# A frequency-filter and mixture-of-experts kernel: six PSUM banks and thinner gating steps in the forward part, expert products in column halves of 64

## The chip, the cores and the metric

The kernel runs on one core of a Trainium2 chip. The metric is the device time of one execution in microseconds; a kernel's time is the median of its runs. The engines are named as in the profile: PE is the matrix engine (PEld its weight loads), DVE the vector engine, ACT the scalar engine, POOL the GpSimd engine, SP the engine that issues most DMAs.

## The reference

Two blocks follow each other. The first multiplies the spectrum of each sequence by a filter, the second sends each row to one of eight experts, of which each takes at most 80 rows.

```python
# x: (8, 2496, 256), filt: (1249, 256) complex
X = np.fft.rfft(x, axis=1)
y = np.fft.irfft(X * F[None], n=2496, axis=1).reshape(19968, 256)
logits = y @ w_gate                      # (256, 8)
expert_idx = np.argmax(logits, axis=1)
probs = softmax(logits)                  # gate_w: the chosen expert's share
for e in range(8):
    tok_idx = np.where(expert_idx == e)[0]
    if len(tok_idx) > 80:                # keep the 80 of the largest gate_w
        tok_idx = tok_idx[np.argpartition(-gate_w[tok_idx], 80)[:80]]
    h = np.maximum(y[tok_idx] @ w1[e], 0.0)          # (80, 256) @ (256, 1024)
    out[tok_idx] = gate_w[tok_idx, None] * (h @ w2[e])   # (80, 1024) @ (1024, 256)
# all other rows of out are zero
```

## The kernel before

The transform of length 2496 is done as 39 times 64 points by products with tables. All matrices are float32, and the trace shows two passes of the PE for each float32 product (a call of 16 products appears as x32). The program has three parts, written out in one order by hand; each engine works through its own instructions in that order.

**Forward part** (a loop over k = 0..79; ten steps make a batch b, r is the step within it). One step holds, on PE, `turn_t(k+1)` (4 transposes, L322, copied by ACT), `stage2(k)` (4 products with the second table, L334) and one piece of `stage1` (L308, copied by ACT L313). DVE makes two products `p` with the filter (L340) of stage 2's result, POOL adds and subtracts them into the spectrum `yt` (L348), and DVE transposes the spectrum for storage (L361). At r = 0 `gates(b-1)` (L385) multiplies the finished spectra of a batch by the gate matrix: 32 columns of weights at a time, in four column strips of the PE. At r = 0 `stage2(k)` stands behind stage 1 and the gates, at all other r ahead of stage 1. `turn_z` (L397) and `logits` follow at r = 2 to 4. For two batches at a time, a *gating* makes softmax and candidates in seven parts (`GATING`: for the third pair of batches at k = 67, 68, 69, 70, 72, 74, 75): maximum `mx` and difference `sh` (DVE L440, L442), exponential `ex` (ACT L444), `first`, `fm`, sum and reciprocal, the key, its transposes `pk` (L475) and the eight largest. Beside it run steps on the first four batches: threshold (k = 54 to 60), `ranks` (62), `codes` (63), lists (64, 65), `row_index` (69, a product of 64 little matrices, L664), `gather_rows` (70 to 73, POOL, L799) and `turn_rows` (75 to 78, DVE, L809). The PSUM of this part is a ring of five banks (`fps`), two banks for gates, `turn_z` and indices (`zps`), one for the rest (`mps`).

**Middle part.** Eight tiles of 128 chosen rows are transformed back: POOL gathers table rows (L799), DVE transposes them (`wt`, L809), and `fill(n)` issues the next n of the 20 products per tile (L816) against a page with the batch's spectrum. Between these stand the last two batches' gating, the final threshold, ranks, lists, `row_index` and the slots.

**Experts.** For each e: `turn(e+2)` (two transposes, L1094), `layer1(e+1)` (16 products of a 128 by 128 weight tile with the 80 rows, L1105), `layer2(e)` (8 products in which the hidden rows are the weights and 256 columns of w2 move, L1119), the scaling by ACT (L1122) and a scatter by POOL (L1124). Layer 1 of expert e+1 stands ahead of layer 2 of expert e. Weights of experts 5 to 7 are loaded once layer 2 of experts 0 to 2 has freed their buffers.

Of the kernel before, what the change touches and what calls it, by code (L numbers as in the profile page):

```python
# [91 lines left out]
def kernel(  # L92
# [158 lines left out]
    with tc.manual_schedule():  # L251
# [10 lines left out]
        fps = pool("fps", 5, PSUM)  # L262
        zps = pool("zps", 1, PSUM)
        mps = pool("mps", 1, PSUM)
# [63 lines left out]
        def stage2(k):  # L328
            h, g = divmod(k, NG)
            cb = h % NDB  # L330
            ps = fps.tile([128, SG, 2, NQ], F32, name=f"pb_{k}", tag="f")
            t = t2.pop(k)
            for i in range(SG):
                nc.tensor.matmul(out=ps[:, i].rearrange("p r q -> p (r q)"), lhsT=t[:, i, :],  # L334
                                 rhs=d_t[:, SG * g + i, :], start=True, stop=True)
            pr = []
# [43 lines left out]
        def gates(b):  # L380
            ps = zps.tile([128, 1024], F32, name=f"pz_{b}", tag="z")
            for p0, pn in ((0, 4), (4, 1)):
                for cb in range(NDB):
                    for j in range(4):
                        nc.tensor.matmul(  # L385
                            out=ps[32 * j:32 * j + 32, 128 * p0:128 * (p0 + pn)].rearrange(
# [4 lines left out]
            st["zt"] = gp.tile([128, 5, 128], F32, name=f"zt_{b}", tag="zt")  # L391
            nc.scalar.copy(out=st["zt"][:].rearrange("p t q -> p (t q)"), in_=ps[:, 0:640])

        def turn_z(b):
            ps = zps.tile([128, 8, 128], F32, name=f"py_{b}", tag="z")
            for t in range(5):
                nc.tensor.transpose(ps[:, t, :], st["zt"][:, t, :], ident[:])  # L397
            for e in range(0, E, 4):
                nc.scalar.copy(
                    out=zs[:, e:e + 4, 0:NS].rearrange("p e (j t) -> p t j e", t=5),  # L400
                    in_=ps[:, 0:5].rearrange("p t (j e) -> p t j e", e=EW)[:, :, :, e:e + 4])
# [24 lines left out]
        def gating(p, part):  # L426
# [11 lines left out]
            if part == 0:  # L438
                mx = row("mx")
                nc.vector.tensor_reduce(out=mx[:], in_=l, axis=AX.X, op=AL.max)  # L440
                st["sh"] = big("sh")
                nc.vector.tensor_tensor(out=st["sh"][:], in0=l, in1=bc(mx[:]), op=AL.subtract)  # L442
                st["ex"] = big("ex")
                nc.scalar.activation(out=st["ex"][:], in_=st["sh"][:], func=AF.Exp)  # L444
            elif part == 1:
# [4 lines left out]
                    op0=AL.is_equal, op1=AL.mult)  # L450
                st["fm"] = row("fm")
                nc.vector.tensor_reduce(out=st["fm"][:], in_=st["first"][:], axis=AX.X,
                                        op=AL.max)
            elif part == 2:
                gw = row("gw")
                nc.vector.tensor_reduce(out=gw[:], in_=st["ex"][:], axis=AX.X, op=AL.add)
                nc.vector.tensor_scalar(out=gw[:], in0=gw[:], scalar1=1e-9, scalar2=None,
                                        op0=AL.add)
                st["gw"] = row("gwr")
                nc.vector.reciprocal(out=st["gw"][:], in_=gw[:])  # L460
            elif part == 3:
# [3 lines left out]
                nc.vector.tensor_tensor(out=key[:, 0:N1, :], in0=oh[:], in1=bc(st["gw"][:]),  # L465
                                        op=AL.mult)
# [5 lines left out]
            elif part == 4:  # L472
# [6 lines left out]
            else:  # L479
                for i in (part - 5,):  # L480
# [4 lines left out]
                if part == 6:  # L485
# [109 lines left out]
        def codes(nb, kept, poff):  # L595
# [13 lines left out]
            nc.vector.max(out=cc[:, 8:16], in_=ff)  # L609
            ci = spt([128, KR], I32, "ci")  # L610
# [46 lines left out]
        def row_index(b0, nb):  # L657
            bn = nb - b0
            bplc, bval = st["bplc"], st["bval"]
            pz = zps.tile([128, 2, 512], F32, name=f"pb_r{nb}", tag="z")  # L660
            pb = pz[:, 0, 0:8 * bn].rearrange("p (v g b) -> p v g b", v=2, g=4)
# [16 lines left out]
            st["pz"] = pz  # L678
# [19 lines left out]
        def slot_lists():  # L698
            eplc, eval_ = st["eplc"], st["eval"]
            pe = st["pz"][:, 1, 0:4 * E].rearrange("p (v e) -> p v e", v=4)  # L700
# [180 lines left out]
        for p, steps in ((0, (25, 26, 27, 28, 30, 32, 33)), (1, (45, 46, 47, 48, 50, 52, 53)),  # L881
                         (2, (67, 68, 69, 70, 72, 74, 75))):
            for part, at in enumerate(steps):
                GATING[at] = p, part

        def early(k):
            if k in GATING:
                gating(*GATING[k])
# [741 lines left out]
```

## Time and profile before

| | us |
|---|---|
| median of 3 runs (436.3, 440.12, 451.39) | 440.12 |
| the profiled execution's own time | 442.61 |
| its span in the trace | 440.7 |
| PE busy | 386.9 (88%) |
| PE weight loads busy (beside PE) | 344.3 (78%) |
| DVE busy | 241.0 (55%) |
| POOL busy | 185.0 (42%) |
| ACT busy | 131.5 (30%) |

The forward part takes about the first 262 us of the span, the middle part runs to 372, the experts' products to 429, and the last scatters end the span. A row of the timeline gives the start and length of a run of like instructions, their count, and in brackets how long the engine had stood still before it and which instruction ended that. Lengths of single PE instructions overlap (the next begins while one drains), so the pace is read from starts, not from lengths.

### The profile page before, as it was taken

The numbers are of one execution on the slowest core, as the hardware profiler recorded it, in microseconds if no ns is written. First come the engines' busy times: TensorE is split into PE (matmuls) and PEld (weight loads), VectorE is DVE, ScalarE is ACT, GpSimd is POOL, SyncE is SP. The second block draws the span as 40 slices with busy tenths as digits, with TensorE's granted clock in tenths as the row PEclk, the third lists the DMA queues.
The fourth block names the chain that finished last, engine by engine and source line by source line (L and its number), as shares of the span: only waits on it lengthen the run. The fifth ranks groups of instructions, "written<-read, shape, count | busy, mean of one in ns | idle before, by whom it ended". The sixth has DMA issues, their size and how long they took to land. (4 is left out here: it accounts for less than half of the span.)

```text
span 440.7 us, 8021 instructions
## 1 busy us (share of the span) xinstructions
PE 386.9 (88%) x3047; PEld 344.3 (78%) x3047; DVE 241.0 (55%) x543; ACT 131.5 (30%) x264; POOL 185.0 (42%) x256
## 2 busy tenths in 40 slices
PE   3969999999999999999979959987939999999990
PEld 3969989898799887988977944776837888989870
DVE  7036567578697677887995792287554410110100
ACT  1524454444454443534443510210130000111110
POOL 7024445354355444553482877030444733401010
PEclk9999999999999999999998988998987999999996
DMA  7998699989889899999789584979499985397000
GB/s 214 215 207 288 162 330 311 311 258 305 267 193 333 242 283 275 357 317 329 189 239 340 161 313 134 312 270 409 147 385 396 348 259 200 78 330 233 9 18 10
DMA packets 42836, 109.95 MB, mean 249 GB/s; under 512 B 5354, under 2 KB 16232, under 8 KB 40920
## 3 DMA queue, kind: packets, MB, share of 16 engines
q1 hardware_dynamic: 37638, 99.03, 70.4%
q0 software_dynamic: 3728, 9.15, 6.4%
q10 hardware_dynamic: 1426, 1.19, 0.8%
q8 instruction: 26, 0.43, 0.4%
q14 instruction: 18, 0.15, 0.1%
HBM read 71.66 MB, written 40.58 MB: 255 GB/s over the span
## 5 line engine op out<-in xcount | busy, mean ns | idle before, releaser
L348 POOL TENSOR_TENSOR yt<-p,p 128x256 f32<-128x256 f32 x160 | 115.7, 746 | 132.5 <-DVE p L340 126.9
L340 DVE TENSOR_TENSOR p<-pb,ft 128x512 f32<-128x512 f32 x160 | 102.1, 679 | 60.9 <-PE pb L334 31.1
L308 PE MATMUL pa<-wf_t,x 117*128 117x120 f32 x704 | 92.8, 280 | 8.2 <-DMA x<-in_x_dram 8.2
L308 PEld LDWEIGHTS pa<-wf_t,x 117*128 117x128 f32 x704 | 87.1, 197 | 8.4 <-issue 7.7
L334 PE MATMUL pb<-d_t,t 128*128 128x128 f32 x640 | 86.8, 279 | 1.6 <-ACT tt L313 1.0
L816 PE MATMUL pr<-page,wt 128*128 128x256 f32 x320 | 77.8, 405 | 9.1 <-DVE wt L809 5.4
L334 PEld LDWEIGHTS pb<-d_t,t 128*128 128x128 f32 x640 | 78.5, 193 | 4.7 <-ACT tt L313 2.2
L816 PEld LDWEIGHTS pr<-page,wt 128*128 128x128 f32 x320 | 64.4, 204 | 19.9 <-issue 7.5
L313 ACT COPY tt<-pa 128x480 f32<-128x480 f32 x96 | 47.9, 516 | 78.1 <-PE pa L308 78.1
L322 PE MATMUL pt<-ident,tt 128*128 128x128 f32 x320 | 49.4, 277 | 5.6 <-ACT tt L313 5.6
L326 ACT COPY t<-pt 128x512 f32<-128x512 f32 x80 | 47.1, 589 | 17.9 <-PE pt L322 16.6
L799 POOL DMA_INDIRECT gt<-rows_tbl,idxr x32 | 33.2, 1036 | 39.8 <-DVE wt L809 23.2
L361 DVE STREAM_TRANSPOSE u<-yt 128x512 f32<-128x512 f32 x70 | 48.9, 699 | 0.0
L322 PEld LDWEIGHTS pt<-ident,tt 128*128 128x128 f32 x320 | 37.2, 143 | 8.2 <-ACT tt L313 6.6
L809 DVE STREAM_TRANSPOSE wt<-gt 128x640 f32<-128x640 f32 x32 | 26.2, 834 | 20.9 <-DMA gt<-rows_tbl,idxr 20.2
L1105 PEld LDWEIGHTS ph_True<-xs_True,w 128*128 128x128 f32 x256 | 29.6, 192 | 0.6
L1105 PE MATMUL ph_True<-xs_True,w 128*128 128x80 f32 x256 | 29.5, 274 | 0.0
L1119 PE MATMUL po_True<-w,hT_True 128*80 128x256 f32 x128 | 28.8, 379 | 0.0
L1110 DVE TENSOR_SCALAR hT_True<-ph_True 128x320 f32<-128x320 f32 x8 | 3.9, 492 | 45.2 <-ACT hT_True L1109 41.5
L1124 POOL DMA_INDIRECT out_dram<-ys_True,idxs x8 | 7.4, 920 | 43.8 <-ACT ys_True L1122 41.2
L820 ACT COPY yr<-pr 128x256 f32<-128x256 f32 x8 | 3.0, 372 | 75.1 <-PE pr L816 66.8
L385 PE MATMUL pz<-yt,wg 128*32 128x512 f32 (+1 forms) x256 | 23.4, 475 | 1.9 <-POOL yt L348 1.1
(187 smaller groups left out, 264.8 us busy)
## 6 DMA issues: line engine op xcount, KB each, us to landing
out_dram<-zero_t SPq DMA_DIRECT2D x32, 624.0 KB
yf<-u SPq DMA_DIRECT2D x56, 320.0 KB
page<-yf SPq DMA_DIRECT2D x28, 640.0 KB
w<-in_moe_w_dram SPq DMA_DIRECT2D x16, 1024.0 KB
x<-in_x_dram SPq DMA_DIRECT2D x16, 936.0 KB
x<-in_x_dram SPq DMA_DIRECT2D x7, 702.0 KB
fst<-in_filt_r_dram SPq DMA_DIRECT2D x10, 128.0 KB
fst<-in_filt_i_dram SPq DMA_DIRECT2D x10, 128.0 KB
```

Of the source, the lines that this page charges most:

```text
L308: nc.tensor.matmul(out=ps[:, j, :], rhs=wf_t, start=True, stop=True, lhsT=xt[3 * b + ch][:, j0 + j - JC * ch, 128 * cb:128 * cb + 128])
L313: nc.scalar.copy(out=tt[h][:, :, H3 * j0:H3 * j0 + hn * jn].rearrange("p s (j h) -> p s j h", h=hn), in_=v)
L322: nc.tensor.transpose(ps[:, i, :], tt[h][:, 2 * s:2 * s + 2, :].rearrange("p r n -> p (r n)"), ident[:])
L326: nc.scalar.copy(out=t2[k][:], in_=ps[:])
L334: nc.tensor.matmul(out=ps[:, i].rearrange("p r q -> p (r q)"), lhsT=t[:, i, :], rhs=d_t[:, SG * g + i, :], start=True, stop=True)
L340: nc.vector.tensor_tensor(out=p, in0=ps[:], in1=f.unsqueeze(2).to_broadcast([128, SG, 2, NQ]), op=AL.mult)
L348: nc.gpsimd.tensor_tensor(out=y[:, :, 2 * r:2 * r + 2, :], in0=a, in1=b, op=op)
L361: nc.vector.transpose(uu[h][:, :, SG * g:SG * g + SG, :].rearrange("p a s w -> p s a w"), spectrum(h)[:, SG * g:SG * g + SG])
L799: nc.gpsimd.indirect_dma_start(out=gts[b, g][:].rearrange("p s q -> p (s q)"), out_offset=None, in_=quarters, in_offset=bass.IndirectOffse ...
L816: nc.tensor.matmul(st["po"][:], lhsT=wts[b][:, s, :], rhs=columns(pages[b], s), start=(s == 0), stop=(s == NS - 1))
L1105: nc.tensor.matmul(ph[:, fc // 4, fc % 4, 0:cap], lhsT=w1[:, k, 128 * fc:128 * fc + 128], rhs=xs[:, k, :], start=(k == 0), stop=(k == NDB ...
L1119: nc.tensor.matmul(po[0:cap, :], lhsT=hT[:, fc, :], rhs=w2[:, fc, :], start=(fc == 0), stop=(fc == NFC - 1))
```

## The change

In the forward part `zps` is gone: `fps` has six banks and `mps` two. `gates`, `turn_z`, `row_index` and the slots' product take one-bank tiles of `fps`; gates and `turn_z` use two of them, for four fifths and one fifth of the columns, each with its own copy. `stage2(k)` always stands right behind `turn_t(k+1)`, so at r = 0 ahead of stage 1 and gates; its products on DVE and POOL (`filtered`) keep their place behind the gates there. The gating is cut into eleven parts; the third pair's now stand at k = 70 to 79. The steps on the first four batches move one to three steps later: threshold to 57 to 63, `ranks` 65, `codes` 66, the fields 67, the lists 68 and 69, `row_index` 71, `gather_rows` 72 to 75, `turn_rows` 76 to 79.

In the middle part `gather_all(2)` and the first eight parts of the last gating stand ahead of the `fill(6)` that ends tile 0, and `row_index` stands after 12 of tile 3's products instead of 19.

In the experts part layer 1 takes weights in column halves of 64, with one bank per half of the hidden columns, and layer 2 of experts 0 to 6 takes 64 columns of w2 as weights and moves the 80 hidden rows. Its result is transposed: DVE copies it (`yT`), and `back(e-1)`, two transposes that stand behind layer 1 of e+1, turns it for scaling and scatter. Expert 7 keeps the old form of layer 2.

```diff
-        fps = pool("fps", 5, PSUM)
-        zps = pool("zps", 1, PSUM)
-        mps = pool("mps", 1, PSUM)
+        fps = pool("fps", 6, PSUM)
+        mps = pool("mps", 2, PSUM)
...
         def gates(b):
-            ps = zps.tile([128, 1024], F32, name=f"pz_{b}", tag="z")
+            st["zt"] = gp.tile([128, 5, 128], F32, name=f"zt_{b}", tag="zt")
             for p0, pn in ((0, 4), (4, 1)):
+                ps = fps.tile([128, 128 * pn], F32, name=f"pz_{b}_{p0}", tag="f")
                 for cb in range(NDB):
...
-        for p, steps in ((0, (25, 26, 27, 28, 30, 32, 33)), (1, (45, 46, 47, 48, 50, 52, 53)),
-                         (2, (67, 68, 69, 70, 72, 74, 75))):
+        for p, steps in ((0, (25, 26, 27, 28, 29, 30, 31, 32, 34, 36, 37)),
+                         (1, (45, 46, 47, 48, 49, 50, 50, 51, 53, 55, 56)),
+                         (2, (70, 70, 71, 72, 72, 73, 74, 75, 77, 78, 79))):
...
                 turn_t(k + 1)
+            ps = stage2(k)
             if r or not b:
-                stage2(k)
+                filtered(k, ps)
             for h, i in s1_steps(k):
                 stage1(h, i)
...
             if b and not r:
                 gates(b - 1)
-                stage2(k)
+                filtered(k, ps)
...
-            if 75 <= k < 79:
-                turn_rows(0, k - 75)
+            if 76 <= k < 80:
+                turn_rows(0, k - 76)
...
-        fill(6)
         turn_all(1)
         load_page(2, keep, "page1", nc.vector.memset)
+        gather_all(2)
+        for part in range(8):
+            gating(3, part)
+        fill(6)
         load_page(3, late, "page0")
-        gather_all(2)
-        for part in range(4):
-            gating(3, part)
         fill(7)
-        gating(3, 4)
+        gating(3, 8)
...
-        fill(19)
+        fill(12)
         row_index(EARLY, B)
         gather_all(4)
-        fill(6)
+        fill(13)
...
-            ph = psF.tile([128, 2, 4, 128], F32, name=f"ph_{first}_{e}", tag="ph")
-            for fc in range(NFC):
-                for k in range(NDB):
-                    nc.tensor.matmul(
-                        ph[:, fc // 4, fc % 4, 0:cap], lhsT=w1[:, k, 128 * fc:128 * fc + 128],
-                        rhs=xs[:, k, :], start=(k == 0), stop=(k == NDB - 1))
+            for m in range(2):
+                ph = psF.tile([128, 4, 128], F32, name=f"ph_{first}_{e}_{m}", tag="ph", bufs=3)
+                for i in range(4):
+                    for k in range(NDB):
+                        for c in (0, 64):
+                            f = 512 * m + 128 * i + c
+                            nc.tensor.matmul(ph[c:c + 64, i, 0:cap], lhsT=w1[:, k, f:f + 64],
+                                             rhs=xs[:, k, :], start=(k == 0),
+                                             stop=(k == NDB - 1))
...
+            if e < E - 1:
+                po = psF.tile([128, NDB, 128], F32, name=f"po_{first}_{e}", tag="po")
+                for d in range(NDB):
+                    for fc in range(NFC):
+                        for c in (0, 64):
+                            nc.tensor.matmul(
+                                po[c:c + 64, d, 0:cap],
+                                lhsT=w2[:, fc, 128 * d + c:128 * d + c + 64], rhs=hT[:, fc, :],
+                                start=(fc == 0), stop=(fc == NFC - 1))
+                yTs[e] = fp.tile([128, NDB, cap], F32, name=f"yT_{first}_{e}", tag="yT")
+                nc.vector.tensor_copy(out=yTs[e][:], in_=po[:, :, 0:cap])
+                return
...
+        def back(e):
+            pb = psF.tile([128, C], F32, name=f"pb_{first}_{e}", tag="pb", bufs=1)
+            for d in range(NDB):
+                nc.tensor.transpose(pb[0:cap, 128 * d:128 * d + 128], yTs[e][:, d, :], ident[:])
```

PE in the experts part, before: one round of the loop (`px` are the turned rows, `ph` layer 1, `po` layer 2).

```order
L1094 MATMUL px_True_3939<-ident,xg_True_3861 128x80 x2
L1119 MATMUL po_True_3944<-w_3262,hT_True_3916 80x256 x8
L1105 MATMUL ph_True_3961<-xs_True_3942,w_3686 128x80 x16
L1094 MATMUL px_True_3981<-ident,xg_True_3865 128x80 x2
L1119 MATMUL po_True_3986<-w_3683,hT_True_3936 80x256 x8
```

The same place after the change.

```order
L1110 MATMUL px_True_3994<-ident,xg_True_3882 128x80 x2
L1143 MATMUL po_True_3999<-hT_True_3920,w_3283 64x80 x32
L1125 MATMUL ph_True_0_4038<-xs_True_3997,w_3708 64x80 x16
L1125 MATMUL ph_True_1_4056<-xs_True_3997,w_3708 64x80 x16
L1159 MATMUL pb_True_4074<-ident,yT_True_4032 80x128 x2
L1110 MATMUL px_True_4082<-ident,xg_True_3886 128x80 x2
L1143 MATMUL po_True_4087<-hT_True_3957,w_3705 64x80 x32
```

Both layers are now 32 products of 64 weight columns with 80 moving columns, and a turn back stands between layer 1 and the next turn.

PE in the forward part around k = 70 (r = 0), before: `pa` is stage 1, `pt` the transposes, `pz` the gates, `pb` stage 2.

```order
L322 MATMUL pt_2768<-ident,tt 128x128 x4
L308 MATMUL pa_1_2775<-wf_t,x_0_2090 128x120 x4
L385 MATMUL pz_2781<-yt,wg 32x512 x8
L385 MATMUL pz_2781<-yt,wg 32x128 x8
L334 MATMUL pb_2800<-d_t,t_70_2671 128x128 x4
L322 MATMUL pt_2819<-ident,tt 128x128 x4
L334 MATMUL pb_2826<-d_t,t_71_2773 128x128 x4
```

And after the change.

```order
L321 MATMUL pt_2697<-ident,tt 128x128 x4
L332 MATMUL pb_2704<-d_t,t_70_2670 128x128 x4
L307 MATMUL pa_1_2709<-wf_t,x_0_2095 128x120 x4
L389 MATMUL pz_0_2716<-yt,wg 32x512 x8
L389 MATMUL pz_4_2726<-yt,wg 32x128 x8
L321 MATMUL pt_2748<-ident,tt 128x128 x4
L332 MATMUL pb_2755<-d_t,t_71_2702 128x128 x4
```

Stage 2 of k = 70 moved from behind the gates to ahead of stage 1; the gates write two tiles.

DVE at the same place, before: `p_69` to `p_71` are the filter's products; the index product's four small steps (`em`, `lo`, `idxr`) stand ahead of `p_70`.

```order
L340 TENSOR_TENSOR p_69_2680<-pb_2673,ft 128x512
L361 STREAM_TRANSPOSE u_2623<-yt 128x4x4x32
L456 TENSOR_REDUCE gw_2692<-ex_2630 128x39
L457 TENSOR_SCALAR gw_2692<-gw_2692 128x39
L460 RECIPROCAL gwr_2695<-gw_2692 128x39
L670 TENSOR_SCALAR em_2763<-pb_r_2697 128x16
L672 TENSOR_SCALAR lo_2762<-pb_r_2697,blk 128x16
L674 SCALAR_TENSOR_TENSOR lo_2762<-pb_r_2697,lo_2762 128x16
L676 TENSOR_TENSOR idxr<-lo_2762,em_2763 128x4x4
L340 TENSOR_TENSOR p_70_2805<-pb_2800,ft 128x512
```

And after the change.

```order
L343 TENSOR_TENSOR p_69_2679<-pb_2672,ft 128x512
L364 STREAM_TRANSPOSE u_2609<-yt 128x4x4x32
L662 TENSOR_TENSOR bplc_2627<-f_t_2621,iota 128x512
L343 TENSOR_TENSOR p_70_2736<-pb_2704,ft 128x512
L343 TENSOR_TENSOR p_70_2738<-pb_2704,ft 128x512
L364 STREAM_TRANSPOSE u_2609<-yt 128x4x4x32
L444 TENSOR_REDUCE mx_2744<-lg 128x39
L447 TENSOR_TENSOR sh_2746<-lg,mx_2744 128x312
L343 TENSOR_TENSOR p_71_2760<-pb_2755,ft 128x512
```

The seven DVE steps of the third gating that stood ahead of `p_70` (`mx` to the reciprocal) now stand behind it, and of the lists `bplc` stands there instead.

## Rows read from the trace of the kernel before

**Rows 1.** The page's head: busy time, share and instructions by engine.
```profile
PE 386.9 (88%) x3047; PEld 344.3 (78%) x3047; DVE 241.0 (55%) x543; ACT 131.5 (30%) x264; POOL 185.0 (42%) x256
```

**Rows 2.** PE's waits, summed: what waited, for what, us, times, longest.
```profile
PE pr L816 <- DVE wt L809: 5.4, 1, 5.4
...
PE pz L385 <- POOL yt L348: 1.1, 2, 0.6
```

**Rows 3.** Windows: busy us by engine, then PE clock, DMA share, GB/s.
```profile
245.00:260.00 15.00, 12.66 (x112) 12.31 (x111) 12.71 (x24) 6.25 (x13) 12.60 (x16) 1.00 0.84 255
...
372.00:429.00 57.00, 56.87 (x397) 48.35 (x396) 5.65 (x15) 6.84 (x16) 12.14 (x13) 1.00 0.41 131
```

**Rows 4.** Timeline of the experts: start, length, engine, line, operation, count.
```profile
371.89 7.31 PE L1105 MATMUL ph_True<-xs_True,w 128*128 128x80 f32 x64
...
414.67 0.30 PE L1094 MATMUL px_True<-ident,xg_True 80*128 80x80 f32 x2
...
414.81 3.62 PE L1119 MATMUL po_True<-w,hT_True 128*80 128x256 f32 x16
...
415.75 0.32 DVE L1097 COPY xs_True<-px_True 128x160 f32<-128x160 f32 x1
...
418.27 3.69 PE L1105 MATMUL ph_True<-xs_True,w 128*128 128x80 f32 x32
...
421.80 7.07 PE L1119 MATMUL po_True<-w,hT_True 128*80 128x256 f32 x32
```

**Rows 5.** Weight loads grouped by shape: busy us, mean ns of one.
```profile
L1105 PEld LDWEIGHTS ph_True<-xs_True,w 128*128 128x128 f32 x256 | 29.6, 192 | 0.6
...
L1119 PEld LDWEIGHTS po_True<-w,hT_True 128*80 128x80 f32 x128 | 18.6, 150 | 7.5
...
L385 PEld LDWEIGHTS pz<-yt,wg 128*32 128x32 f32 x256 | 8.3, 112 | 16.1 <-issue 9.7 <-POOL yt L348 4.5 <-PE pa L308 0.9
```

**Rows 6.** Timeline of PE around the gates of one batch.
```profile
143.02 2.37 PE L385 MATMUL pz<-yt,wg 128*32 128x512 f32 x32
145.32 1.16 PE L334 MATMUL pb<-d_t,t 128*128 128x128 f32 x8
...
146.75 1.06 PE L334 MATMUL pb<-d_t,t 128*128 128x128 f32 x8
```

**Rows 7.** Timeline of PE, DVE and ACT from k = 67 to 70.
```profile
228.57 0.43 DVE L440 TENSOR_REDUCE mx<-lg 128x39 f32<-128x312 f32 x1
...
229.56 0.46 ACT L444 ACTIVATE ex<-sh 128x312 f32<-128x312 f32 x1 [3.22 <-DVE sh L442]
...
231.20 1.12 PE L322 MATMUL pt<-ident,tt 128*128 128x128 f32 x4 [2.36 <-ACT tt L313]
...
232.11 1.92 PE L334 MATMUL pb<-d_t,t 128*128 128x128 f32 x8
...
235.11 0.66 PE L664 MATMUL pb_r<-bval,bplc 128*32 128x32 bf16 x64
...
237.06 0.40 DVE L460 RECIPROCAL gwr<-gw 128x39 f32<-128x39 f32 x1
...
237.98 2.36 PE L385 MATMUL pz<-yt,wg 128*32 128x512 f32 x32 [0.73 <-DVE lo L674]
...
241.54 1.29 DVE L340 TENSOR_TENSOR p<-pb,ft 128x512 f32<-128x512 f32 x2 [3.49 <-PE pb L334]
```

**Rows 8.** Timeline at the end of the forward part.
```profile
262.10 0.82 DVE L809 STREAM_TRANSPOSE wt<-gt 128x640 f32<-128x640 f32 x1
...
263.06 5.46 PE L816 MATMUL pr<-page,wt 128*128 128x256 f32 x12 [5.40 <-DVE wt L809]
```

**Rows 9.** Timeline of the middle part: the last gating, then tile 4.
```profile
287.21 0.52 PE L475 MATMUL pk<-ident,key 128*128 128x128 f32 x3 [0.70 <-DVE key L465]
...
328.15 1.70 DVE L809 STREAM_TRANSPOSE wt<-gt 128x640 f32<-128x640 f32 x2 [0.80 <-DMA gt<-rows_tbl,idxr]
...
332.20 4.13 PE L816 MATMUL pr<-page,wt 128*128 128x256 f32 x9
```

More of the change, by code (lines that the diff above doesn't have):

```diff
@@ L390, in gates @@
                             start=(cb == 0), stop=(cb == NDB - 1))
-            st["zt"] = gp.tile([128, 5, 128], F32, name=f"zt_{b}", tag="zt")
-            nc.scalar.copy(out=st["zt"][:].rearrange("p t q -> p (t q)"), in_=ps[:, 0:640])
+                nc.scalar.copy(
+                    out=st["zt"][:, p0:p0 + pn].rearrange("p t q -> p (t q)"), in_=ps[:])
         def turn_z(b):
[L395 to L398, printed above, removed]
+            for p0, pn in ((0, 4), (4, 1)):
+                ps = fps.tile([128, pn, 128], F32, name=f"py_{b}_{p0}", tag="f")
+                for t in range(pn):
+                    nc.tensor.transpose(ps[:, t, :], st["zt"][:, p0 + t, :], ident[:])
                 nc.scalar.copy(
-                    out=zs[:, e:e + 4, 0:NS].rearrange("p e (j t) -> p t j e", t=5),
-                    in_=ps[:, 0:5].rearrange("p t (j e) -> p t j e", e=EW)[:, :, :, e:e + 4])
+                    out=zs[:, :, 0:NS].rearrange("p e (j t) -> p t j e", t=5)[:, p0:p0 + pn],
+                    in_=ps[:].rearrange("p t (j e) -> p t j e", e=EW)[:, :, :, 0:E])
         def logits(b, part):
@@ L450, in gating @@
                     op0=AL.is_equal, op1=AL.mult)
+            elif part == 3:
                 st["fm"] = row("fm")
@@ L453, in gating @@
                                         op=AL.max)
[L454 to L458, printed above, removed]
+            elif part == 4:
+                st["sum"] = row("gw")
+                nc.vector.tensor_reduce(out=st["sum"][:], in_=st["ex"][:], axis=AX.X,
+                                        op=AL.add)
+            elif part == 5:
+                nc.vector.tensor_scalar(out=st["sum"][:], in0=st["sum"][:], scalar1=1e-9,
+                                        scalar2=None, op0=AL.add)
                 st["gw"] = row("gwr")
-                nc.vector.reciprocal(out=st["gw"][:], in_=gw[:])
-            elif part == 3:
+                nc.vector.reciprocal(out=st["gw"][:], in_=st["sum"][:])
+            elif part == 6:
                 oh = st["sh"]
@@ L464, in gating @@
                                         op=AL.is_equal)
-                nc.vector.tensor_tensor(out=key[:, 0:N1, :], in0=oh[:], in1=bc(st["gw"][:]),
-                                        op=AL.mult)
+            elif part == 7:
+                nc.vector.tensor_tensor(out=key[:, 0:N1, :], in0=st["sh"][:],
+                                        in1=bc(st["gw"][:]), op=AL.mult)
                 nc.sync.dma_start(
@@ L479, in gating @@
             else:
-                for i in (part - 5,):
+                for i in (part - 9,):
                     b = 2 * p + i
@@ L1072, in experts @@
     def experts(fp, psF, load, first):
-        xgs, xss, hTs = {}, {}, {}
+        xgs, xss, hTs, yTs = {}, {}, {}, {}
         near = NH if first else 0
         def gather(e):
-            xg = fp.tile([cap, C], F32, name=f"xg_{first}_{e}", tag="xg", bufs=E)
+            xg = fp.tile([cap, C], F32, name=f"xg_{first}_{e}", tag="xg", bufs=E - near)
             nc.gpsimd.indirect_dma_start(
@@ L1139, in experts @@
                 layer1(e + 1)
+            if e > 0:
+                back(e - 1)
             if e + 2 < E:
```

88 lines of the change are left out of this document (51 added, 37 removed).

## The prediction

> **What bounds the kernel now.** I began with the page's head: PE is busy for 386.9 us, 88% of the span, no other engine for more than 241.0 [rows 1]. So a gain must come from PE's own work or from the few places where PE stands still. The waits of PE give the second sort: 5.4 us in one piece for DVE at the end of the forward part, and small ones at the gates, such as 1.1 us for POOL [rows 2]. The windows give the first sort. From 372 to 429 us PE is busy for 56.87 of 57.0 us at the full clock (2.4 GHz), with DMA at 0.41, while DVE works for 5.65 and ACT for 6.84 us [rows 3]. The reader should see that the experts are pure PE work: nothing but fewer or shorter passes shortens them. From 245 to 260 us DVE is busy for 12.71 of 15 us and POOL for 12.60, beside PE's 12.66: the tail of the forward part has three engines near their limit.
>
> **The experts.** The timeline gives the price of a pass. Layer 2 of experts 6 and 7 runs 32 passes of 256 moving columns in 7.07 us, 0.221 us each or 0.863 ns a column [rows 4]. Layer 1 starts at 418.27 and layer 2 follows at 421.80: 32 passes of 80 columns in 3.53 us, 0.110 each, though 80 columns by that slope ask for only 0.069. What fills the rest is the load. The mean load lasts 112 ns for 32 columns, 150 for 80 and 192 for 128 [rows 5]: 0.83 ns a column on a fixed 85 ns that overlaps. So 128 columns occupy 0.107 us, which is layer 1's pace: the load is hidden behind the pass before it, and is longer than it. Layer 2 is the opposite case: loads of 80 columns (0.067) behind passes of 0.221.
>
> In halves of 64 columns a load occupies 0.053 us and a pass of 80 columns 0.069, so the pass is the longer one. Each layer is 64 such passes. If the two halves run abreast they are 32 pairs at p = 0.070 us: 2.24 us a layer in place of 3.53 and 3.6. That different column strips run abreast is seen at the gates: 16 passes of 512 and 16 of 128 columns, which at 0.863 ns would take 8.8 us in a row, take 2.37 us in four strips [rows 6]. There the weights have 32 columns; two strips of 64 the trace doesn't show, so I bound p: 0.053 (loads alone) below, twice 0.069 = 0.138 (no overlap) above. I take 0.070, because the gates are the nearest rows and use the same kind of strips.
>
> The sum for the experts after: 15 half-layers are 480 pairs, 33.6 us. Expert 7's layer 2 in the old form, 7.07 / 2 = 3.5. Six turns at 0.14 (414.67 to 414.81): 0.8. Seven turns back, each two passes of 128 columns at 0.11: 1.5. Changes between strips and the whole array: a stage 2 right behind the gates takes 1.16 us, elsewhere 1.06 [rows 6], so 0.1 each, two a round: 1.4. Behind the last halves `back(6)` has no layer 1 ahead of it and waits for the copy `yT`, 0.32 us by a copy of the same size [rows 4] plus the hand-over both ways: 0.6. Together 480p + 7.8 = 41.4 us in place of 57.0 (371.89 to 428.87): **-15.5 us**. The other copies `yT` lie under layer 1, as DVE is idle there.
>
> The Trainium skill, "TensorEngine Tiling (Array Packing)", Key Properties, says that a change of tiling mode drains TensorE; the trace agrees, with about 0.1 us a change.
>
> Weights stay hidden: a round falls from 7.1 to about 5.1 us, DMA's share in this window is 0.41 now, and each of the last three loads is asked for three rounds before its layer 1, 15 us.
>
> **The forward part.** Around k = 68 one chain of waits is seen. `ex` stands in ACT's queue and waits 3.22 us for DVE's `sh`; behind it stands the copy that the next transposes need, and PE stands still for 2.36 us [rows 7]. After that pause the next stage 2 takes 1.92 us in place of 1.06 [rows 6, 7], at the lower of the two clocks (1.2 GHz); for the stage 1 behind it I add 0.3. Together 3.5 us. The gates then wait 0.73 us for the index product's copy, which freed their bank, and elsewhere 1.1 for POOL [rows 2, 7]. The change puts `ex` a step after `sh`, and the gates in other banks, so these 5.3 us of PE waits are the most that PE itself can get back.
>
> But what ends the forward part is DVE: PE waits 5.40 us at 263.06 for the last `wt`, which DVE begins at 262.10 [rows 8]. So the gain is DVE's. DVE starts the product of k = 70 at 241.54, after 3.49 us of idling for stage 2 behind the gates [rows 7]. After the change that product can start earlier by the stall (3.5), the wait (0.73), the gates (2.36) and the stage 1 and index product that stood ahead of it (8 passes of 0.11 and 0.66 [rows 7]): at 233.4. DVE has more of its own to do before it (list work that now falls into k = 66 to 69), so I take 234.5. From there DVE had 262.92 - 241.54 = 21.4 us to the end of `wt`, of which 2.3 idle in the window [rows 3]. Behind k = 70 come, in addition, the seven gating steps from `mx` to the reciprocal, 0.4 to 0.7 us each [rows 7], 3.5 us, and the index copies, 0.7. That ends at 234.5 + 21.4 + 4.2 = 260.1, and tile 0's products start at 260.2 in place of 263.06: **-3 us**. The bounds: -1, if the four `wt`, which now stand one step later, each add a wait for POOL or their gather; -6, if DVE's 2.3 us of idling and the slow passes behind PE's long wait vanish too. PE loses at the gates of k = 70, which now come before POOL has finished the spectrum of k = 69, about 1.7 us; it is hidden as long as DVE ends the part.
>
> The extra copies of gates and `turn_z` cost ACT about 0.3 us a batch, hidden, as ACT is busy for 30% of the span [rows 1].
>
> **The middle part.** `ex` no longer waits behind a tile's copy on ACT, so the key is ready earlier; PE waits 0.70 us for it [rows 9], and that goes. `row_index` stands 7 products earlier, 14 passes of 0.22, so the gathers of tile 4 start about 3 us earlier, and the 0.80 us that DVE waits for them ahead of tile 4's `wt` goes. With some 0.3 us lost to changes of order: **-1.2 us**, bounds 0 and -1.5. Tile 4's products, from 332.20, and all behind them move with it.
>
> **The sum.** -15.5 - 3 - 1.2 = -19.7 on the profiled execution's 442.6: 422.9. The profiled execution lies 2.5 us above the median, so against the median 440.1 it is 420.4; I say 421.
>
> **The rivals.**
> *The halves share the array's time* (no overlap). Then p = 0.138, the experts take 480 x 0.138 + 7.8 = 74.0 us, +17.0, and the rest keeps -4.2: 440.1 + 12.8 = 453, slower by 3%. It decides from p = 0.129 on; the gates' 2.37 us speaks against it.
> *A load doesn't hide behind passes* of the same or the other half. Then a pair costs 0.053 + 0.069 = 0.122 at least, the experts 66.4, +9.4, and the time is 445. The same comes near if two loads of 64 take as long as one of 128 (0.107 to 0.112: about 57 to 60 us for the experts, 436 to 439). For it: layer 1 is at the pace of its loads now. Against it: layer 2's loads of 0.067 don't show behind its passes, and the gates' four loads begin within one pass.
> The Trainium skill, "TensorE: Matmul & The Clock Gate", Part 3, says that a load overlaps running matmuls only when their row groups differ. By that rule this rival holds, as both halves use all rows, and the forecast would be 445; the trace disagrees, with layer 1's pace of 0.110 us where a load and a pass in a row ask for 0.107 + 0.069.
> *The gain outside the experts goes into new waits.* DVE and POOL lag through the tail with the gating's steps behind k = 70, tile 0 starts no earlier, and the last gathers come a step later. The experts' gain stays: 440.1 - 15.5 + 0 to 3 = 425 to 428. For it: DVE 12.71 and POOL 12.60 of 15 us.
> *More comes back in the forward part*, -6 or more with the slow-clock passes: 412 to 417.
>
> **How the numbers follow.** Forecast (experts as summed, -2 to -6 elsewhere) 0.63: 417 to 424. New waits 0.18: 424 to 430. More back 0.07: 410 to 417. Loads not hidden 0.08: 436 to 447. No overlap 0.04: about 453. The time is that of the likeliest, 421. The range 412 to 431 leaves out the last two and the far end of *more back*, about 0.14. A measurement of this kernel tells about 2% from no change, so 431.3 and 448.9 are the borders: faster 0.88, same 0.08, slower 0.04.
>
> **What would show it.** In the experts, a layer of 32 products should take 2.2 to 2.4 us from start to start, a round about 5.1, and the whole 41 to 43; 3.5 a layer would mean that loads set the pace, 4.4 that the halves don't overlap. Around k = 68 to 70 the wait of the transposes for ACT should be gone, with a wait of the gates for POOL of 1 to 2 us in its place. Tile 0's first products should start near 260, tile 4's 4 us earlier than 332. If the experts last more than 47 us, or tile 0 starts after 263, the forecast's steps are wrong.

## The result, and the profile after

The changed kernel takes 424.78 us (median of 4 runs, 423.76 to 427.07) against 439.44 for the kernel before beside it: a ratio of 0.971, 95% interval 0.964 to 0.977. Faster, as forecast, inside the range of 412 to 431 and 3.8 us above the 421 foretold. A kernel's executions fall into a faster and a slower group; ratios compare the faster ones alone, and the trace of `exp_only` below is of a slower one (442.09 us, where its faster ones took 432.3 to 438.6). Between the two profiled executions the span falls by 17.0 us (440.7 to 423.7); the forecast was 19.7.

The head of the page after, to be read against [rows 1]:

```profile
span 423.7 us, 9235 instructions
PE 368.7 (87%) x3653; PEld 334.1 (79%) x3653; DVE 241.7 (57%) x550; ACT 131.8 (31%) x272; POOL 185.3 (44%) x256
```

PE lost 18.2 us of work while its instructions grew by 606. Its largest waits, against [rows 2]:

```profile
PE pa L307 <- DMA x<-in_x_dram: 9.9, 2, 7.5
PE pr L828 <- DVE ones_f L984: 9.0, 1, 9.0
...
PE pt L321 <- ACT tt L312: 3.7, 9, 0.5
...
PE pz L389 <- POOL yt L351: 0.6, 1, 0.6
```

The wait at the end of the forward part (named after the instruction behind the last `wt`) grew from 5.4 to 9.0 us: PE arrives earlier, DVE doesn't. The longest wait of the transposes for ACT fell from 2.4 to 0.5.

The timeline of the experts, against [rows 4] (L1125 layer 1, L1143 layer 2, L1159 the turn back, L1110 the next turn, L1152 the old form):

```profile
367.53 4.65 PE L1125 MATMUL ph_True<-xs_True,w 128*64 128x80 f32 x128
367.88 0.94 POOL L1094 DMA_INDIRECT xg_True<-y_sel,idxg  x1 [3.07 <-PE px_True L1107]
...
372.10 0.36 PE L1110 MATMUL px_True<-ident,xg_True 80*128 80x80 f32 x2
...
372.39 2.44 PE L1143 MATMUL po_True<-hT_True,w 128*64 128x80 f32 x64
...
374.65 2.38 PE L1125 MATMUL ph_True<-xs_True,w 128*64 128x80 f32 x64
...
376.97 0.42 PE L1159 MATMUL pb_True<-ident,yT_True 128*80 128x128 f32 x2
...
377.22 0.30 PE L1110 MATMUL px_True<-ident,xg_True 80*128 80x80 f32 x2
...
377.45 2.44 PE L1143 MATMUL po_True<-hT_True,w 128*64 128x80 f32 x64
...
379.72 2.38 PE L1125 MATMUL ph_True<-xs_True,w 128*64 128x80 f32 x64
...
390.64 0.91 POOL L1167 DMA_INDIRECT out_dram<-ys_True,idxs  x1 [5.41 <-issue]
390.69 2.17 PE L1125 MATMUL ph_True<-xs_True,w 128*64 128x80 f32 x57 [0.41 <-issue]
...
396.39 2.37 PE L1125 MATMUL ph_True<-xs_True,w 128*64 128x80 f32 x62 [0.55 <-issue]
...
407.05 0.39 PE L1159 MATMUL pb_True<-ident,yT_True 128*80 128x128 f32 x2 [0.52 <-DVE yT_True L1148]
...
407.28 3.62 PE L1152 MATMUL po_True<-w,hT_True 128*80 128x256 f32 x16
...
410.98 0.47 ACT L1165 ACTIVATE ys_True<-po_True,gate 80x256 f32<-80x256 f32 x1 [2.98 <-PE po_True L1152]
...
412.58 0.91 POOL L1167 DMA_INDIRECT out_dram<-ys_True,idxs  x1 [3.40 <-ACTq L1272]
```

The first two layers take 4.57 us (from 367.53 until the turn begins at 372.10) for 64 pairs: 0.0714 us a pair. A round (377.45 less 372.39) takes 5.06 us. The experts last 43.4 us (to 410.89) in place of 57.0. A wait named issue is one in which the engine waited for nothing that the profile shows. The rows at 367.88 and 390.64 are POOL's first gather of the experts' rows and one of its scatters.

Where the 17.0 us are, from starts in the two traces:

| stretch | before | after | gain | forecast |
|---|---|---|---|---|
| to tile 0's first product | 263.06 | 262.92 | 0.1 | 3 |
| tile 0 to the experts' first product | 108.83 | 104.61 | 4.2 | 1.2 |
| the experts' products | 57.0 | 43.4 | 13.6 | 15.5 |
| behind them | 11.8 | 12.8 | -1.0 | 0 |

These are two single executions, and parts that no edit touched differ between traces too. The changed forward part brings tile 0 at 262.04 to 263.82 (six traces), that of before at 263.06 and 264.97. From tile 0 to the experts it is 104.5 to 105.7 us with the changed middle part (four traces), 108.8 and 106.6 with that of before (the 264.97 and the 106.6 are those of `exp_only_spread`, below). So the first line says that the forecast 3 us didn't come, not that the gain is 0.1, and the 4.2 of the second can't all be put down to the change. The experts' stretch is steady: 43.4 and 43.1 us in the two traces of the changed kernel, 57.0 in both traces with the old form.

### The profile page after: what moved, and what is told of

The parts are those of the page before. It is cut to its first block, busy times and chain, and to the rows that moved or that the text cites. A ratio compares the mean times of both kernels' runs of the same rounds, so it can differ in the third digit from the quotient of the medians.

```text
span 423.7 us, 9235 instructions
## 1 busy us (share of the span) xinstructions
PE 368.7 (87%) x3653; PEld 334.1 (79%) x3653; DVE 241.7 (57%) x550; ACT 131.8 (31%) x272; POOL 185.3 (44%) x256
## 5 line engine op out<-in xcount | busy, mean ns | idle before, releaser
L307 PE MATMUL pa<-wf_t,x 117*128 117x120 f32 x704 | 94.1, 282 | 9.9 <-DMA x<-in_x_dram 9.9
L307 PEld LDWEIGHTS pa<-wf_t,x 117*128 117x128 f32 x704 | 88.4, 200 | 10.2 <-issue 10.1
L828 PE MATMUL pr<-page,wt 128*128 128x256 f32 x320 | 76.6, 401 | 12.1 <-DVE ones_f L984 9.0
L332 PE MATMUL pb<-d_t,t 128*128 128x128 f32 x640 | 85.5, 277 | 0.1
L821 DVE STREAM_TRANSPOSE wt<-gt 128x640 f32<-128x640 f32 x32 | 25.9, 831 | 19.4 <-DMA gt<-rows_tbl,idxr 19.2
L389 PE MATMUL pz<-yt,wg 128*32 128x512 f32 (+1 forms) x256 | 22.3, 474 | 0.6 <-POOL yt L351 0.6
L1125 PE MATMUL ph_True<-xs_True,w 128*64 128x80 f32 x512 | 19.5, 233 | 1.0 <-issue 1.0
L1125 PEld LDWEIGHTS ph_True<-xs_True,w 128*64 128x64 f32 x512 | 18.4, 137 | 1.4 <-issue 1.3
L389 PEld LDWEIGHTS pz<-yt,wg 128*32 128x32 f32 x256 | 7.7, 111 | 14.1 <-issue 10.8
L1143 PE MATMUL po_True<-hT_True,w 128*64 128x80 f32 x448 | 17.0, 234 | 0.0
```

Of the source, the lines that this page charges most:

```text
L307: nc.tensor.matmul(out=ps[:, j, :], rhs=wf_t, start=True, stop=True, lhsT=xt[3 * b + ch][:, j0 + j - JC * ch, 128 * cb:128 * cb + 128])
L389: nc.tensor.matmul(out=ps[32 * j:32 * j + 32].rearrange("p (s a q) -> p s a q", a=4, q=32), lhsT=wg[:, cb, :], rhs=spectrum(2 * b + cb)[:, ...
L828: nc.tensor.matmul(st["po"][:], lhsT=wts[b][:, s, :], rhs=columns(pages[b], s), start=(s == 0), stop=(s == NS - 1))
L1125: nc.tensor.matmul(ph[c:c + 64, i, 0:cap], lhsT=w1[:, k, f:f + 64], rhs=xs[:, k, :], start=(k == 0), stop=(k == NDB - 1))
```

## The experiments

All ratios are to the kernel before, run beside each kernel on the same chip. A kernel without a ratio was run once, for its trace.

**The two halves of the change alone.** `exp_only` is the kernel before with the function `experts` of the changed kernel; `rest_only` is the changed kernel with the function of before.

> The kernel before with the experts part of the change alone. Theory (the experts are PE work of their own and independent of what lies ahead): their stretch falls from 57.0 to about 43.4 us as in the changed kernel, the end is about 13 us earlier (ratio 0.971), and tile 0 and the experts' start stay where they were (263 and 372 us). Rival (part of the gain needs the rest of the change, or is lost again in the last scatters): ratio above 0.98.

> The changed kernel with the experts part of before. Theory: forward and middle part gain about 4.4 us together, nearly all of it behind tile 0's first products: tile 0 starts at 263, the experts at 367.5, ratio 0.990. By the prediction's step tile 0 would start at 260 and the ratio be the same, 0.99; the two differ in where the gain stands.

`rest_only` gave 0.995 (0.991 to 1.000): tile 0 at 262.58, the experts at 368.28, so the gain stands where the first theory put it, behind tile 0. Up to the experts it is 3.6 us, not 4.4. `exp_only` gave 0.988 (0.984 to 0.993): the theory's 0.971 falls, and the number is the rival's. The experts' form alone bought less than half of what it buys in the changed kernel. What ate it is neither the rest of the change nor, beyond the 1.0 us behind the experts, the scatters. In its trace the experts take 52.1 us, with 3.4 us of waits named issue in the first two layers; the trace of another kernel, `candidates_late`, shows the same.

**The strips' order.** `halves_in_turn` does the same products in another order:

```diff
-                for i in range(4):
-                    for k in range(NDB):
-                        for c in (0, 64):
+                for c in (0, 64):
+                    for i in range(4):
+                        for k in range(NDB):
...
-                    for fc in range(NFC):
-                        for c in (0, 64):
+                    for c in (0, 64):
+                        for fc in range(NFC):
```

> The changed kernel with the same half products, but all of one column half ahead of all of the other (8 calls of a half, then 8 of the other), so that neighbours in PE's order use the same strip. Theory (the gain comes from the two strips running abreast): a pass of 80 columns follows its neighbour after 0.069 us, a layer takes 4.4 to 4.6 us in place of 2.26, the experts 76 us, the end 32 us later than the changed kernel, at about 456. Rival (the gain comes from smaller loads, whatever the order): a layer of 2.3 us, no change. Second rival (loads of the same strip don't hide): 7.8 us a layer, the experts 125 us.

Timeline of PE, one round:

```profile
385.47 0.28 PE L1125 MATMUL ph_True<-xs_True,w 128*64 128x80 f32 x1
385.53 0.23 PE L1143 MATMUL po_True<-hT_True,w 128*64 128x80 f32 x1
385.59 0.23 PE L1125 MATMUL ph_True<-xs_True,w 128*64 128x80 f32 x1
385.60 0.23 PE L1143 MATMUL po_True<-hT_True,w 128*64 128x80 f32 x1
...
385.73 3.72 PE L1125 MATMUL ph_True<-xs_True,w 128*64 128x80 f32 x61
389.38 0.42 PE L1159 MATMUL pb_True<-ident,yT_True 128*80 128x128 f32 x2
...
389.87 3.77 PE L1143 MATMUL po_True<-hT_True,w 128*64 128x80 f32 x61
393.42 0.28 PE L1125 MATMUL ph_True<-xs_True,w 128*64 128x80 f32 x1
```

A layer takes 3.6 us (389.87 to the next layer's 393.42 is 3.55), where the alternating order takes 2.26. So the order decides, and smaller loads alone bring nothing over before's 3.53. It is not 4.4: where the strip changes, PE begins the next strip's passes while the last ones of the other still run, as the rows from 385.47 to 385.60 show, in which layer 2 and layer 1 alternate 0.01 to 0.06 us apart. Within one strip a pass starts 0.069 us after the one ahead of it, as the theory has it; the overlap at the changes is what it left out. The experts took 69.4 us, the time was 451.4 beside 441.0 before. Of the 69.4, 13.2 are the first two layers, some 6 more than twice 3.55: the wait described under the next headings stands there too.

**The end of the forward part.** `candidates_late` takes the last two parts of the third gating out of k = 78 and 79:

```diff
-                         (2, (70, 70, 71, 72, 72, 73, 74, 75, 77, 78, 79))):
+                         (2, (70, 70, 71, 72, 72, 73, 74, 75, 77))):
...
         assert not todo_y and not turns
+        gating(2, 9)
+        gating(2, 10)
```

> The changed kernel with the last two parts of the third gating (each batch's eight largest, 2.6 us of DVE) behind the loop, after the last wt. Theory (DVE's own work ends the forward part): tile 0 starts about 2.4 us earlier, at 260.5, and the end comes 2 us earlier (ratio 0.966). Rival (gathers or POOL end it): tile 0 within 0.7 us of 262.9, ratio as the changed kernel's 0.971.

Tile 0 started at 260.77, as the theory has it. But in `candidates_late_spread` below, whose forward part is the same, it started at 262.48, where the rival has it. The two differ in when PE leaves the loop, 253.28 and 254.31 at the last stage 2. Counted from there tile 0 comes 7.5 and 8.2 us later, and 9.2 to 10.2 in the seven traces with the two parts inside the changed loop: DVE's own work sets the length of the end, as the theory says, but how late PE gets there differs between the two by 1.0 us. The ratio was 0.983 (0.976 to 0.990), worse than the changed kernel's 0.971 (0.964 to 0.977). PE's sum of waits and its timeline at the experts' start:

```profile
PE ph_True L1127 <- issue: 4.6, 7, 1.1
```

```profile
367.28 2.09 PE L1127 MATMUL ph_True<-xs_True,w 128*64 128x80 f32 x51
369.73 0.36 PE L1127 MATMUL ph_True<-xs_True,w 128*64 128x80 f32 x3 [0.36 <-issue]
370.44 0.41 PE L1127 MATMUL ph_True<-xs_True,w 128*64 128x80 f32 x5 [0.36 <-issue]
371.87 0.36 PE L1127 MATMUL ph_True<-xs_True,w 128*64 128x80 f32 x4 [1.02 <-issue]
373.28 0.37 PE L1127 MATMUL ph_True<-xs_True,w 128*64 128x80 f32 x4 [1.06 <-issue]
374.71 3.95 PE L1127 MATMUL ph_True<-xs_True,w 128*64 128x80 f32 x61 [1.06 <-issue]
```

From 369.4 to 374.7 PE does three to five passes (with their loads some 8 instructions) every 0.7 or 1.4 us, waiting for nothing that the profile names; then it goes on at the lower clock (1.2 GHz; a mean of 0.56 of full speed is granted from 374.7 to 378.6, 1.00 until then, after PE had been busy for 1.5 of 5.3 us). The experts take 49.9 us in place of 43.4. In the changed kernel's trace the same place is unbroken. What stands beside it are POOL's six gathers of the experts' rows, which run from 366.25 to 373.5 here.

**Is it chance?** The changed kernel once more, and three kernels with the gathers spread out:

```diff
-            xg = fp.tile([cap, C], F32, name=f"xg_{first}_{e}", tag="xg", bufs=E - near)
+            xg = fp.tile([cap, C], F32, name=f"xg_{first}_{e}", tag="xg", bufs=2 if first else E)
...
-        for e in range(near, E):
+        for e in range(near, near + 2 if first else E):
             gather(e)
...
             if e + 2 < E:
                 turn(e + 2)
+            if first and e + 4 < E:
+                gather(e + 4)
```

> The changed kernel once more, unaltered. In candidates_late PE stood still in the first two layers of the experts for 3.8 us in pieces (bursts of some 8 instructions 0.7 us apart, waits named issue), in the changed kernel's first profile not at all. Theory (whether PE's instructions arrive in time hangs on when the six gathers of the experts' rows fall against them, so on the build, not on chance): again no such wait in the first two layers, experts 43.4 us, ratio 0.970. Rival (chance of each execution): ratio between 0.970 and 0.985 with a wide spread.

> candidates_late with the gathers of the experts' rows spread out: two ahead of the experts, each other one behind a turn, from a ring of two buffers, in place of six at once. Theory (the gathers' transfers hold up the transfer of PE's instructions): no wait named issue in the first two layers, experts 43 to 44 us in place of 49.9, the end 6 us earlier, ratio 0.967. Rival (PE's instruction supply is short by itself at this rate): the same waits at the same place, ratio 0.983.

> exp_only with the gathers spread in the same way. Theory: its waits named issue in the first two layers (3.4 us) go, experts 43 to 45 us in place of 52.1, span near 427 to 432. Rival: as exp_only.

`after_again`: 0.970 (0.965 to 0.975), no such wait in the first two layers, experts 43.1 us. `candidates_late_spread`: 0.963 (0.958 to 0.968), experts 44.0 us, the first two layers unbroken:

```profile
366.86 4.65 PE L1127 MATMUL ph_True<-xs_True,w 128*64 128x80 f32 x128
```

`exp_only_spread`: first two layers unbroken, experts 45.1 us, 431.6 us beside 439.1 (tile 0 started 1.9 us later than before, with the same forward part). So the wait in the first two layers goes when the gathers are spread, in all three kernels that have them so (the third is `both_late_spread` below). With six gathers at once it stood in the traces of six of the seven kernels with the new experts, those below that were run once included; the one that escapes, twice, is the changed kernel. There the first gather starts 0.35 and 0.27 us behind the first product (367.88 against 367.53); in the six others between 0.11 us behind and 1.12 us ahead of it. That this decides is not shown: no run moved the gathers alone.

That PE waits for its own instructions I infer from the bursts of 8, from what removes the wait, and from `before` and `rest_only`, which have no such wait beside the same six gathers, at 18 PE instructions per microsecond. How the gathers do it stays open. The profile counts transfers of instructions as DMA queues of their own (q8 and q14). In `candidates_late` none of these started from 354 to 375.7 us, and PE goes on at 374.7, so what it waits for there is not the next one of them; the theory's "transfer of PE's instructions" is not shown. Waits of the same name, 0.2 to 1.6 us long, also stand in later layers, whether the gathers are at once (1.0 us in all in the changed kernel) or spread (1.6 to 2.5); no run tells their cause.

**The forward part's transfers.** `zeros_late` moves four zero-fills of the output from k = 50 to 57 to ACT's queue behind the loop; `both_late_spread` is that with `candidates_late_spread`:

```diff
-    def put_zeros(n, todo=None):
+    def put_zeros(n, todo=None, queue=None):
...
-            nc.sync.dma_start(
+            (queue or nc.sync).dma_start(
...
-            if (1 <= b <= 5 and r in (0, 2, 5, 7)) or 6 <= k < 10 or k in (60, 62, 64, 66, 67, 68, 69, 70):
+            if (1 <= b <= 4 and r in (0, 2, 5, 7)) or 6 <= k < 10 or k in (60, 62, 64, 66, 67, 68, 69, 70):
...
         assert not todo_y and not turns
+        put_zeros(4, queue=nc.scalar)
```

> candidates_late_spread and, besides, the four zero-fills of the output at k = 50 to 57 moved behind the loop, to ACT's queue. Theory (PE's gain up to k = 57, 6.8 us, is given back at k = 58 because the transfer of x comes no earlier, beside zero-fills on a DMA at 0.99): the wait for x at k = 58, 2.5 us with 1.2 of slow passes behind it, goes or halves, and tile 0 starts 2 us earlier still, at 258.7; ratio 0.962. Rival (DVE and POOL end the forward part whatever PE does): the wait for x falls, tile 0 stays at 260.8, ratio as candidates_late_spread.

> The changed kernel with only the four zero-fills of k = 50 to 57 moved behind the loop (gathers and gating as in the changed kernel). Theory (the transfer of x sets when PE can go on at k = 58, and DVE follows PE): the wait for x at k = 58 nearly goes, PE leaves the loop about 4.5 us earlier than in the changed kernel (249 in place of 253.7), and tile 0 starts 4 us earlier, at 258.7 to 259. Rival (DVE's own work ends the forward part, and what both_late_spread gained there, 6.6 us, is the candidates' 2.6 us and chance): tile 0 at 262 or later.

At k = 58 the changed kernel waits for x, and its next stage 2 runs at the lower clock (granted 0.50; 1.92 us, elsewhere 1.06); in the kernel before the same wait is 0.53 us:

```profile
192.95 2.89 PE L307 MATMUL pa<-wf_t,x 117*128 117x120 f32 x12 [2.46 <-DMA x<-in_x_dram]
...
197.13 1.92 PE L332 MATMUL pb<-d_t,t 128*128 128x128 f32 x8
```

```profile
197.81 1.57 PE L308 MATMUL pa<-wf_t,x 117*128 117x120 f32 x12 [0.53 <-DMA x<-in_x_dram]
```

With the zero-fills moved (`zeros_late`) the wait is short, the last stage 2 starts 5.2 us earlier than in the changed kernel (247.59, 252.80) and tile 0 6.1 us, more than the 4 expected:

```profile
191.36 1.57 PE L307 MATMUL pa<-wf_t,x 117*128 117x120 f32 x12 [0.49 <-DMA x<-in_x_dram]
...
256.83 5.21 PE L828 MATMUL pr<-page,wt 128*128 128x256 f32 x12 [8.08 <-issue]
```

`both_late_spread` has tile 0 at 256.27, not at the 258.7 expected: of its gain there nearly all is the zero-fills', and the 0.6 us beyond `zeros_late` are less than executions differ. It takes 421.49 us, ratio 0.959 (0.956 to 0.963), beside 0.970 for the changed kernel in the same comparison: faster than both kernels of this case, by 1% than the changed one. `zeros_late` alone, with the six gathers at once, gave 428.0 (before: 441.1), since its experts took 50.5 us.

**The middle part.** `gating_behind_fill` puts the last gating, with the gathers of tile 2 ahead of it, back behind the `fill(6)`; `row_index_19` puts `fill(19)` and `fill(6)` back around `row_index`.

> The changed kernel with the last gating behind the fill that ends tile 0, as before. Theory (that move brings the key about 1 us, since the exponential no longer stands behind the tile's copy on ACT): from turn_z of the last batch to the last pk 10.5 us in place of 9.6, the experts start 0.5 to 1 us later against tile 0's start. Rival (worth nothing): 9.6 us.

> The changed kernel with row_index behind 19 of tile 3's products as before, in place of 12. Theory (its gathers come 3 us later, and with them tile 4 by 0.5 to 1.5 us): from tile 3's first products to tile 4's 25.1 to 26 us in place of 24.6. Rival (tile 4 waits for other things): 24.6 us.

`gating_behind_fill`: 10.24 us from `turn_z` to `pk` in place of 9.61, as the theory has it in kind, and PE waits for the key again:

```profile
283.82 0.52 PE L485 MATMUL pk<-ident,key 128*128 128x128 f32 x3 [0.44 <-DVE key L475]
```

From tile 1 to tile 2 it takes 11.26 us; the changed kernel takes 10.64, as do the other traces with its order there (10.63 or 10.64), and before 11.53. `row_index_19`: 26.5 us from tile 3 to tile 4 in place of 24.6, beyond the theory's upper end. In eight of nine traces with the changed order there it is 24.6 (in `both_late_spread` 25.9):

```profile
304.08 9.33 PE L828 MATMUL pr<-page,wt 128*128 128x256 f32 x28 [2.75 <-DVE place L607]
...
330.59 4.76 PE L828 MATMUL pr<-page,wt 128*128 128x256 f32 x13
```

## Why the prediction was right, and where its terms were off

**Experts: the mechanism holds, the gain was 1.9 us smaller than summed.** The two strips of 64 run abreast; the pair costs 0.0714 us where 0.070 was taken (480 pairs: 0.7 us), and the sum had nothing for waits named issue. Two of them (0.41 us before 390.69, 0.55 before 396.39) stand in two layers that last 2.94 and 3.15 us where the others last 2.3: 1.5 in all. That covers the difference. Both rivals of this part fall: without overlap a pair would be near 0.138, with loads in the open 0.122. `halves_in_turn` shows what the first would have looked like, in part. One price of the second rival was summed wrong: for pairs of 0.107 to 0.112 us, 480p + 7.8 gives 59.2 to 61.6 us and 438 to 440.5, not 57 to 60 and 436 to 439. The rule of the Trainium skill, "TensorE: Matmul & The Clock Gate", Part 3, that a load overlaps running matmuls only when their row groups differ, would have made the time 445; the trace doesn't bear it out here, with 0.0714 us a pair where a load and a pass in a row ask for 0.122.

What the forecast did not see is that this form asks for three times as many PE instructions per microsecond (64 passes and 64 loads in 2.26 us, before 32 and 32 in 3.53), and that six gathers beside its start can cost it 6.5 us. The changed kernel had none of that in either trace. A prediction of `exp_only` by the same sum would have been wrong by 10 us.

**Behind the experts: a term that was missing.** The last scatter starts 1.1 us after its rows are scaled (410.98 + 0.47 to 412.58), before 0.3 us:

```profile
428.96 0.47 ACT L1122 ACTIVATE ys_True<-po_True,gate 80x256 f32<-80x256 f32 x1 [3.03 <-PE po_True L1119]
429.70 0.91 POOL L1124 DMA_INDIRECT out_dram<-ys_True,idxs  x1 [2.59 <-ACTq L1227]
```

The turn back is not the reason, for `halves_in_turn` has the same one, and its last scatter comes after 0.3 us as well:

```profile
437.87 0.47 ACT L1165 ACTIVATE ys_True<-po_True,gate 80x256 f32<-80x256 f32 x1 [2.98 <-PE po_True L1152]
438.61 0.91 POOL L1167 DMA_INDIRECT out_dram<-ys_True,idxs  x1 [2.54 <-ACT ys_True L1165]
```

There, and in the kernel before, all eight scatters start 0.3 to 0.4 us after their rows are ready. In the ten traces in which the halves alternate, five or six of the eight start 0.4 to 4.5 us after. At 390.64 POOL ends such a wait within 0.05 us of PE's. So the lateness goes with the alternating halves, not with the turn back. They bring more PE instructions per microsecond and also shorter rounds (5.1 us, before 7.1, `halves_in_turn` 8.0); which of the two makes POOL late stays open.

**Forward part: the step failed, though its first half was met.** DVE took up the product of k = 70 at 234.40, as forecast (234.5), and PE left the loop 3.7 us earlier (the last stage 2 at 252.80, before 256.51). Then DVE needed 28.4 us to the end of the last `wt` (262.77) where 25.6 were summed. DVE's timeline there, and tile 0's first products:

```profile
234.40 1.27 DVE L343 TENSOR_TENSOR p<-pb,ft 128x512 f32<-128x512 f32 x2
...
247.20 1.29 DVE L343 TENSOR_TENSOR p<-pb,ft 128x512 f32<-128x512 f32 x2 [1.40 <-PE pb L332]
...
255.63 0.84 DVE L821 STREAM_TRANSPOSE wt<-gt 128x640 f32<-128x640 f32 x1 [1.45 <-DMA gt<-rows_tbl,idxr]
...
261.94 0.83 DVE L821 STREAM_TRANSPOSE wt<-gt 128x640 f32<-128x640 f32 x1
...
262.92 5.33 PE L828 MATMUL pr<-page,wt 128*128 128x256 f32 x12 [8.96 <-DVE ones_f L984]
```

The same stretch as a window (busy us by engine: PE, PEld, DVE, ACT, POOL; then PE clock, DMA share, GB/s), first before, then after:

```profile
241.54:262.92 21.38, 16.12 (x144) 15.77 (x141) 19.06 (x34) 7.92 (x16) 16.48 (x21) 0.97 0.78 254
```

```profile
234.40:262.77 28.37, 18.93 (x229) 17.53 (x226) 23.74 (x48) 9.13 (x19) 21.73 (x31) 0.91 0.75 251
```

DVE's work grew by 4.7 us, 0.5 more than summed, but its idle time doubled, from 2.3 to 4.6 us; a wait of 1.40 us for stage 2 and one of 1.45 for a gather are the largest pieces. The failed step is that it took DVE's old idle time as enough for the new order. The larger miss lies earlier. The prediction looked at k = 67 to 70 alone. Thin gating and the gates' own banks save about 3 us at each of the first two gatings too: by k = 58 PE is 6.8 us ahead of the kernel before. At k = 58 it gives 3.7 of them back in the wait for x, and at k = 66 only 0.9 are left. `rest_only` was 8.6 us ahead there, kept 2.2 and then 0.5. The wait of 0.53 us in the trace of before was the sign that x had no slack. `zeros_late` shows what hangs on it: with that wait at 0.49 us PE ends the loop 5.2 us earlier, and tile 0 follows by 6.1. What the moved fills free for other transfers isn't separated from that.

**Middle part: right in kind; 2 us are shown where 1.2 were summed.** Of the 4.2 us, 1.1 lie between tile 3 and tile 4, where `row_index_19` loses 1.9. There the step counted only a wait of 0.80 us; the four `wt` take 3.0 us unbroken from 322.04, before 4.2 from 325.62. About 0.9 lie between tile 1 and tile 2, where PE no longer waits 0.70 us for the key; `gating_behind_fill` loses 0.6 of it. From tile 2 to tile 3 the changed kernel gained 0.5 and behind tile 4 it lost 0.4, but both stretches differ by as much between traces of the same code (11.17 and 11.72 us from tile 2 to tile 3 in the changed kernel's own two). The other 2.2 lie ahead of tile 1 and aren't shown to be the change's: `exp_only_spread`, with the middle part of before, needs 17.2 us from tile 0 to tile 1, the changed kernel 18.1, before 20.3. In the kernel before, ACT's copy of the last gates starts 2.5 us after the gates end; in the changed kernel at once. But in `exp_only_spread`, whose forward and middle parts are those of before, it starts at once too:

```profile
275.72 0.69 ACT L392 COPY zt<-pz 128x640 f32<-128x640 f32 x1 [19.27 <-remote]
```

```profile
274.09 0.69 ACT L392 COPY zt<-pz 128x640 f32<-128x640 f32 x1 [15.70 <-PE pz L385]
```

The first row is of before, the second of `exp_only_spread`. What ACT waits for in the first stays open.

**What of the number is luck.** The total missed by 2.7 us (17.0 for 19.7), less than its parts did: the forward part brought 2.9 us less than summed and the middle part 3.0 more, of which the 2.2 ahead of tile 1 aren't the change's as far as is shown. The measured 424.78 lies just above the forecast's own band (417 to 424), in that of the rival *the gain outside the experts goes into new waits*; tile 0 no earlier is its account of the forward part, and the one that the trace bears out.

## What to carry to other kernels

Where a product moves few columns past wide weights, put the weights in column halves and let neighbouring instructions alternate between the halves: here the pace fell from that of the load to that of the pass, and without the alternating order the halving brought nothing. A form with many short instructions may be held up where the profile names no reason, so look for waits named issue and keep bursts of small gathers away from its start. A part in which PE gets ahead gains only as far as the input's transfer has slack: even a small wait for it in the trace of before says where the gain may be given back. And before a microsecond of one stretch is put down to an edit, compare the stretch between traces in which nothing in it was changed.

## What the runs showed of the hardware that was not expected

PE in the halved form, at 57 instructions per us, fell to bursts of some 8 instructions 0.7 or 1.4 us apart while six gathers ran, and lost 6.5 us in 49.9 (`candidates_late`); with two gathers at a time it didn't. At 36 per us (`halves_in_turn`) it was hit too, at 18 (`before`, `rest_only`) not. The two traces that were spared with six gathers at once have the first gather 0.27 and 0.35 us behind the first product, the six that were hit at most 0.11 us behind; whether that is the cause was not tried. POOL's scatters were late by up to 4.5 us where the halves alternate, and on time in `halves_in_turn`. And passes of two different strips overlap even in a program that does one strip after the other, for some passes around each change of strip.
